# Attention and gated network on one core: part of the weight bit-packing moved to ScalarE, plain products in another order, packs at other places

## The chip, the cores and the metric

The kernel runs on one core of a Trainium2 chip. The metric is the device time of one execution in microseconds (us). The engines are named as in the profile: PE (TensorE matmul), PEld (TensorE weight load), DVE (VectorE), ACT (ScalarE), POOL (GpSimd) and SP (SyncE, which here only issues DMAs). Each engine works through its own instructions in program order.

## The reference

Eight batches, eight heads, 576 positions and head size 64 go through a windowed attention: the first four heads see the last 32 positions, the other four every fourth of the last 128. The result, 4608 rows of 512, goes through a gated network with 1536 inner columns.

```python
scores = scale * np.matmul(q, k.transpose(0, 1, 3, 2))
scores = np.where(masks[None], scores, -1e9)
attn = exp(scores - max) / (sum + 1e-09);  x = (attn @ v)      # rows of 8 heads x 64 = 512
g = x @ w_gate;  silu = g * (1.0 / (1.0 + np.exp(-g)))
val = x @ w_val
out = (silu * val) @ w_out
```

q, k and v are float32; the three weight matrices are float64, and reach the chip as pairs of 32-bit words (a low and a high word).

## The kernel before, in words

**Chunks and steps.** The 4608 rows are twelve chunks of 384 columns (x is held transposed). The first four chunks are "plain": twelve steps each, 48 steps `s` in all, one step for each block of 128 inner columns. A step is 36 matmuls of 128x128 by 128x384: `gv_mm(.., 0)`, the gate, 12 matmuls into the bank `bg` (L401); `gv_mm(.., 1)`, the value, 12 into `bv` (L401); and `out_mm(s - 1)`, the output product of the step before, 12 into four banks `bo` (L439). Every operand is split into a high and a low float32r part, and a product is three matmuls: high by high, high weight by low x, low weight by high x. The last eight chunks run in pairs through a scheme with seven products in place of eight (L713); nothing of the change lies there.

**Between the products of a step.** ACT takes the tanh of the gate (`act_tanh`, L411), DVE multiplies it by the gate (`dve_u`, L416), which frees `bg`, and then by the value (`dve_h`, L421), which frees `bv`; ACT makes the high part of h (`h_hi`, L426) and POOL the low part (`h_lo`, L431), which `out_mm` reads. `bg` and `bv` are single banks, so the gate of step s + 1 waits for `dve_u` of step s, and the value of step s + 1 for `dve_h` of step s.

**Weights.** The weights of a step are two units, 24 units in all, 2s and 2s + 1 for step s. The gate reads unit 2s alone, the value reads both, the output product unit 2s + 1. A unit passes through stages: a load of 768 KB into one of six raw buffers (`w_load`, issued by SP, as soon as the unit that held the buffer has passed stage B); stage E, `w_exp`, on ACT (L205), which rescales the high word in place; stage B, `w_bits`, on DVE, two instructions: the high word shifted left by 3 (L212), then the low word shifted right by 29 and or-ed in (L213); stage H, `w_split_hi`, the float32r high part, on ACT (L221); stage L, `w_split_lo`, the low part, on POOL (L225). All this is done in the first plain chunk; afterwards the weights stay in place.

**What sets the order.** The first four attention packs (chunk 0) and the first units are written out by hand as a string of stages (`first`, for PE, DVE and ACT). After that the steps are written in a loop, in which `w_upto` says up to which unit each stage is written there, and `tc.issue_after` holds the weight work behind `dve_u` or `dve_h`; a scheduler turns what is written into one fixed order for each engine. Attention packs for later chunks are put between the products at numbered slots (`visits`, three slots to a step): a visit "A" computes the results of one pack and the scores of the next, a visit "B" turns them (transposes), and copies x.

## Time and profile before

| | us |
|---|---|
| runs (3): median, lowest, highest | 963.69, 962.80, 965.67 |
| the profiled execution | 964.01 |
| its span, first to last instruction | 962.2 |
| PE busy in the span | 942.5 |
| DVE, ACT, POOL busy | 672.3, 397.7, 375.5 |

The span is 1.8 us shorter than the execution's own time. A busy share is a mean over stages with different limits; the opening (0 to 20 us: attention of chunk 0), the weight stage (20 to 118 us: plain chunk 0 with the 24 units) and all that follows are read apart.

### The profile page before, as it was taken

The numbers are of one execution on the slowest core, as the hardware profiler recorded it, in microseconds if no ns is written. First come the engines' busy times: TensorE is split into PE (matmuls) and PEld (weight loads), VectorE is DVE, ScalarE is ACT, GpSimd is POOL, SyncE is SP. The second block draws the span as 40 slices with busy tenths as digits, with TensorE's granted clock in tenths as the row PEclk, the third lists the DMA queues.
The fourth block names the chain that finished last, engine by engine and source line by source line (L and its number), as shares of the span: only waits on it lengthen the run. The fifth ranks groups of instructions, "written<-read, shape, count | busy, mean of one in ns | idle before, by whom it ended". The sixth has DMA issues, their size and how long they took to land.

```text
span 962.2 us, 23928 instructions
## 1 busy us (share of the span) xinstructions
PE 942.5 (98%) x9960; PEld 915.5 (95%) x9960; DVE 672.3 (70%) x1180; ACT 397.7 (41%) x776; POOL 375.5 (39%) x460
## 2 busy tenths in 40 slices
PE   7899899999999999999999999999999999999998
PEld 6788899999999999999999999999999999999998
DVE  5878655667677655677699487779487789466583
ACT  4664432232333333444546334445334447234352
POOL 1566411111111131334367343455343448354472
PEclk9999999999999999999999999999999999999999
DMA  9774345556766791898979988889988878988873
GB/s 368 304 250 146 129 147 183 195 202 230 242 207 225 240 354 35 262 291 270 294 239 290 344 273 279 259 259 309 333 263 280 275 235 260 307 255 253 258 232 122
DMA packets 86060, 238.12 MB, mean 247 GB/s; under 512 B 8768, under 2 KB 29120, under 8 KB 85952
## 3 DMA queue, kind: packets, MB, share of 16 engines
q0 software_dynamic: 36288, 132.14, 44.1%
q1 hardware_dynamic: 36848, 65.07, 19.1%
q10 hardware_dynamic: 12816, 39.38, 12.3%
q8 instruction: 79, 1.29, 0.6%
q14 instruction: 29, 0.24, 0.1%
HBM read 194.08 MB, written 42.47 MB: 246 GB/s over the span
## 4 chain that ended last, share of the span: by engine, by line
PE 88%; DVE 6%; issue 2%; ACT 2%; DMA 1%; POOL 0%; ACTq 0%; POOLq 0%; SPq 0%; DVEq 0%
PE bo L713 30%; PE bg L713 11%; PE bv L713 11%; PE bv L401 9%; PE bo L439 9%; PE bg L401 9%; PE two L339 3%; PE two L299 2%; DVE at_int L213 1%; PE two L323 1%; PE two L357 1%; DVE at_int L212 1%; DVE at_float32r L672 1%; DMA at_int<-w 1%; ACT at_int L205 1%
## 5 line engine op out<-in xcount | busy, mean ns | idle before, releaser
L713 PE MATMUL bo<-at_float32r,at_float32r 128*128 128x384 f32 x1728 | 318.5, 336 | 0.0
L713 PEld LDWEIGHTS bo<-at_float32r,at_float32r 128*128 128x128 f32 x1728 | 299.8, 188 | 1.0
L645 POOL DMA_DIRECT2D at_float32r<-pieces x252 | 137.8, 547 | 242.4 <-PE bo L713 140.1
L672 DVE TENSOR_TENSOR at_float<-bo,at_float 128x384 f32<-128x384 f32 x224 | 122.0, 552 | 101.5 <-PE bo L713 52.2
L431 POOL TENSOR_TENSOR at_float32r<-at_float,at_float32r 128x384 fp32r<-128x384 f32 x48 | 57.4, 1195 | 214.3 <-PE bo L439 173.6
L713 PE MATMUL bg<-at_float32r,at_float32r 128*128 128x384 f32 x648 | 137.0, 337 | 0.0
L713 PE MATMUL bv<-at_float32r,at_float32r 128*128 128x384 f32 x648 | 136.5, 336 | 0.0
L401 PE MATMUL bv<-at_float32r,at_float32r 128*128 128x384 f32 x576 | 112.5, 342 | 3.0 <-ACT at_float32r L221 1.8
L713 PEld LDWEIGHTS bv<-at_float32r,at_float32r 128*128 128x128 f32 x648 | 114.1, 188 | 0.5
L713 PEld LDWEIGHTS bg<-at_float32r,at_float32r 128*128 128x128 f32 x648 | 113.8, 188 | 0.7
L401 PE MATMUL bg<-at_float32r,at_float32r 128*128 128x384 f32 x576 | 111.5, 340 | 2.7 <-DVE at_float L416 1.2
L439 PE MATMUL bo<-at_float32r,at_float32r 128*128 128x384 f32 x576 | 110.1, 338 | 3.2 <-POOL at_float32r L431 2.9
L672 DVE TENSOR_TENSOR at_float32r<-at_float,at_float32r 128x384 fp32r<-128x384 f32 (+1 forms) x112 | 99.9, 914 | 17.9 <-ACT at_float32r L702 14.0
L702 ACT CAST at_float32r<-at_float 128x384 fp32r<-128x384 f32 x168 | 83.1, 512 | 66.7 <-PE bv L713 22.9
L672 POOL TENSOR_TENSOR at_float32r<-at_float,at_float32r 128x384 fp32r<-128x384 f32 x84 | 91.5, 1090 | 43.9 <-ACT at_float32r L702 42.8
L401 PEld LDWEIGHTS bv<-at_float32r,at_float32r 128*128 128x128 f32 x576 | 100.7, 189 | 5.2 <-ACT at_float32r L221 2.1
L401 PEld LDWEIGHTS bg<-at_float32r,at_float32r 128*128 128x128 f32 x576 | 100.2, 188 | 4.8 <-DVE at_float L416 1.8
L439 PEld LDWEIGHTS bo<-at_float32r,at_float32r 128*128 128x128 f32 x576 | 100.3, 188 | 4.5 <-POOL at_float32r L431 3.5
L739 ACT ACTIVATE at_float<-at_float 128x384 f32<-128x384 f32 x96 | 50.6, 527 | 99.3 <-DVE at_float L672 94.6
L416 DVE SCALAR_TENSOR_TENSOR at_float<-at_float,bg 128x384 f32<-128x384 f32 x48 | 26.5, 552 | 71.5 <-ACT at_float L411 71.5
L718 ACT COPY at_float<-bg 128x384 f32<-128x384 f32 x84 | 40.1, 478 | 81.1 <-PE bg L713 81.0
L672 DVE TENSOR_TENSOR at_float<-at_float,at_float 128x384 f32<-128x384 f32 (+1 forms) x64 | 54.6, 878 | 25.1 <-POOL at_float32r L672 11.3
(78 smaller groups left out, 994.4 us busy)
## 6 DMA issues: line engine op xcount, KB each, us to landing
at_float32r<-pieces POOLq DMA_DIRECT2D x252, 512.0 KB, 4.8
pieces<-at_float32r SPq DMA_DIRECT2D x126, 256.0 KB, 3.5
at_int<-w SPq DMA_DIRECT2D x24, 768.0 KB, 6.2
at_float<-vb ACTq DMA_DIRECT2D x36, 390.0 KB, 5.1
out<-at_float SPq DMA_DIRECT2D x48, 192.0 KB, 4.7
at_float<-qkb ACTq DMA_DIRECT2D x14, 448.0 KB, 6.3
at_float<-qkb ACTq DMA_DIRECT2D x15, 400.0 KB, 5.6
at_float<-qkb ACTq DMA_DIRECT2D x7, 640.0 KB, 6.5
```

What stands on the lines that cost most here:

```text
L299: nc.tensor.matmul(out=two[BQ * j:BQ * j + BQ, h, a + BK * g:a + BK * g + BK], lhsT=t[r, q:q + BQ], rhs=t[r, k:k + BK], start=not masked, ...
L339: nc.tensor.matmul(out=two[BQ * j:BQ * j + BQ, h, (D + 1) * g:(D + 1) * (g + 1)], lhsT=t[r, BQ * i:BQ * i + BQ], rhs=v[r, i, :], start=Tru ...
L401: nc.tensor.matmul(out=bank[:, :CH], lhsT=wcol(f, o, low), rhs=x[k], start=n == 0, stop=n == 3 * NK - 1)
L416: last["h"] = nc.vector.scalar_tensor_tensor(out=t, in0=t, scalar=1.0, in1=bank_g[:, :CH], op0=ALU.add, op1=ALU.mult)
L431: nc.gpsimd.tensor_tensor(out=hl, in0=hst[i][0], in1=hst[i][1], op=ALU.subtract)
L439: nc.tensor.matmul(out=bank_o[j][:, :CH], lhsT=wcol(f, 2 * DM + P * j, low), rhs=x, start=f == 0 and n == 0, stop=f == NF - 1 and n == 2)
L645: nc.gpsimd.dma_start(out=taken[asked], in_=pieces[asked % NPIECE])
L672: engine.tensor_tensor(out=out, in0=a, in1=b, op=op)
L702: nc.scalar.copy(out=o[:, 0], in_=src)
L713: nc.tensor.matmul(out=bank, lhsT=w, rhs=x, start=first and n == 0 and t in FRESH, stop=last and n == len(ops) - 1, skip_group_check=True)
L718: nc.scalar.copy(out=kept[KEPT[t]][r], in_=banks[0][r][:, :CH])
L739: nc.scalar.activation(out=f, in_=g, func=AF.Tanh, scale=0.5)
```

## The change

There are five edits.

1. Stage B is cut in two. A new stage T (`w_shift`) comes ahead of it. For the units 1, 2 and 5, 7, 9 .. 23 (12 of the 24), T is one ACT instruction that multiplies the low word by about 2^-29 and rounds it, in place, and B is a single DVE instruction (high word shifted left by 3, or-ed with the low word). For the other 12 units T and B are the two DVE instructions of before.
2. In `gv_mm` the four matmuls with the low weight part come last, after the eight with the high part.
3. In `out_mm` the eight matmuls with the high part of h come first (two for each bank), the four with the low part of h last.
4. The string of the first stages is written in another order: T and B of unit 0 apart, the results of pack 1 behind the exp of pack 3, unit 2's E earlier, and B of unit 3 and E of units 4 and 5 at the end.
5. The visits of packs 4 to 8 lie at slots 5, 11, 18, 24, 31 (A) and 8, 14, 21, 27, 34 (B) in place of 2, 9, 16, 23, 30 and 6, 13, 20, 27, 33.

```diff
+    STAGES = "ETBHL"
...
-    def w_bits(u):
+    def by_act(u):
+        return u in (1, 2) or u > 3 and u % 2 == 1
+
+    def w_parts(u):
+        return [wst[u][k].rearrange("p (a b) -> p a b", a=3) for k in ("lo", "hi")]
+
+    def w_shift(u):
         n = u - NU + NLAST
         y = at(M_LATE + 4 * WU + YW * (u % 3) if n < 0 else M_SPARE if n == 0 else raw_at[(u + 1) % 4], YW, I32)
...
+        if by_act(u):
+            x = wst[u]["lo"]
+            nc.scalar.activation(out=x, in_=x.bitcast(U32), func=AF.Copy, scale=(1 - 2.0 ** -8) * 2.0 ** -29,
+                                 bias=-0.5 + 7.5 * 2.0 ** -8)
+        else:
+            nc.vector.tensor_scalar(out=wst[u]["y"], in0=w_parts(u)[1], scalar1=3, scalar2=None,
+                                    op0=ALU.logical_shift_left)
+
+    def w_bits(u):
+        y = wst[u]["y"]
+        lo, hi = w_parts(u)
+        if by_act(u):
+            nc.vector.scalar_tensor_tensor(out=y, in0=hi, scalar=3, in1=lo,
+                                           op0=ALU.logical_shift_left, op1=ALU.bitwise_or)
+        else:
+            nc.vector.scalar_tensor_tensor(out=y, in0=lo, scalar=29, in1=y,
+                                           op0=ALU.logical_shift_right, op1=ALU.bitwise_or)
         wst[u] = y
...
     def gv_mm(ci, f, which):
...
-        for j, k in enumerate(ORDER):
+        ops = [(j, 0, x) for j in range(NK) for x in (xh, xl)] + [(j, 1, xh) for j in range(NK)]
...
     def out_mm(i):
...
-        for j in range(4):
-            for n, (low, x) in enumerate(((0, hh), (1, hh), (0, hl))):
+        for j, low, x in [(j, low, hh) for j in range(4) for low in range(2)] + [(j, 0, hl) for j in range(4)]:
...
-        for what in ("Q0 Q1 S0 X0 T0 S1 K0 X1 A0 M0 W0 Q2 N0 T1 K1 S2 X2 Q3 A1 W0 W1 U0 W2 W3 S3 X3 N1 T2 H0 L0 T3 K2 A2 "
-                     "W1 K3 U1 N2 H1 A3 W2 L1 W3 U2 N3 H2 U3 L2 H3 L3 W0 W1 W2 W0 W1").split():
+        for what in ("Q0 Q1 S0 X0 T0 S1 K0 X1 A0 M0 W0 Q2 N0 T1 K1 S2 X2 Q3 W1 W0 S3 X3 A1 U0 N1 W2 T2 K2 H0 L0 W3 W4 "
+                     "T3 A2 K3 W1 U1 N2 A3 H1 L1 W0 W2 U2 N3 W3 H2 U3 L2 W4 H3 L3 W1 W0 W2 W1 W2 W3 W0 W0").split():
...
-        visits(4 + n, 2 + 7 * n, 5 + 7 * n + (n < 4))
+        visits(4 + n, 5 + 13 * n // 2, 8 + 13 * n // 2)
...
-            w_upto(B=W + 5)
+            w_upto(T=W + 5, B=W + 5)
```

What this makes of the order is seen at three places. In the rows, `at_1536_int` are raw weight buffers (in place for E and T), `at_776_int` the packed units, `at_1536_float32r` the split weights and `at_384_float` h. The changed kernel's line numbers are its own: L207 is E, L225 T on ACT, L228 T on DVE, L238 and L235 B (of a unit with T on DVE and on ACT), L246 H, L437 the tanh, L442 `dve_u`, L447 `dve_h`, L452 `h_hi`, L404 the low part of x.

DVE in step 7, from `dve_u` to the next `dve_u`, before:

```order
L416 SCALAR_TENSOR_TENSOR at_384_float_672<-at_384_float_672,bg 128x384
L212 TENSOR_SCALAR at_776_int_362<-at_1536_int_167 128x3x256
L213 SCALAR_TENSOR_TENSOR at_776_int_362<-at_1536_int_167,at_776_int_362 128x3x256
L421 SCALAR_TENSOR_TENSOR at_384_float_672<-at_384_float_672,bv 128x384
L212 TENSOR_SCALAR at_776_int_418<-at_1536_int_173 128x3x256
L213 SCALAR_TENSOR_TENSOR at_776_int_418<-at_1536_int_173,at_776_int_418 128x3x256
```

The same step after the change:

```order
L442 SCALAR_TENSOR_TENSOR at_384_float_630<-at_384_float_630,bg 128x384
L228 TENSOR_SCALAR at_776_int_337<-at_1536_int_167 128x3x256
L238 SCALAR_TENSOR_TENSOR at_776_int_337<-at_1536_int_167,at_776_int_337 128x3x256
L404 TENSOR_TENSOR at_384_float32r<-two,at_384_float32r 128x384
L447 SCALAR_TENSOR_TENSOR at_384_float_630<-at_384_float_630,bv 128x384
L235 SCALAR_TENSOR_TENSOR at_776_int_419<-at_1536_int_173 128x3x256
```

The odd unit's T is gone from DVE; a low part of x stands here now because of the later visit.

ACT around the tanh of step 1 (the second L411), before:

```order
L426 CAST at_384_float32r<-at_384_float_586 128x384
L221 CAST at_1536_float32r<-at_776_int_418 128x768
L205 ACTIVATE at_1536_int_167<-at_1536_int_167 128x768
L411 ACTIVATE at_384_float_672<-bg 128x384
L221 CAST at_1536_float32r<-at_776_int_362 128x768
```

And after:

```order
L452 CAST at_384_float32r<-at_384_float_586 128x384
L225 ACTIVATE at_1536_int_380<-at_1536_int_380 128x768
L246 CAST at_1536_float32r<-at_776_int_419 128x768
L207 ACTIVATE at_1536_int_167<-at_1536_int_167 128x768
L246 CAST at_1536_float32r<-at_776_int_471 128x768
L207 ACTIVATE at_1536_int_173<-at_1536_int_173 128x768
L437 ACTIVATE at_384_float_630<-bg 128x384
```

Ahead of this tanh now stand T of unit 5, H of units 4 and 5 and E of units 6 and 7; before, H of unit 3 and E of unit 6.

ACT around the tanh of step 8, where E of the last two units (22 and 23, raw buffers 167 and 173) stands, before:

```order
L205 ACTIVATE at_1536_int_167<-at_1536_int_167 128x768
L275 DMA at_1280_float_514<-qkb 128x896
L411 ACTIVATE at_384_float_586<-bg 128x384
L319 ACTIVATE at_384_float_850<-at_384_float_850 128x384
L205 ACTIVATE at_1536_int_173<-at_1536_int_173 128x768
```

And after:

```order
L207 ACTIVATE at_1536_int_167<-at_1536_int_167 128x768
L437 ACTIVATE at_384_float_586<-bg 128x384
L308 DMA at_780_float_891<-vb 128x780
L207 ACTIVATE at_1536_int_173<-at_1536_int_173 128x768
L302 DMA at_1280_float_516<-qkb 128x896
L246 CAST at_1536_float32r<-at_776_int_1275 128x768
L346 ACTIVATE at_384_float_887<-at_384_float_887 128x384
```

The exp of pack 7 (L319, L346) stood ahead of E of unit 23 and now stands behind it. The order of SP's DMA issues is the same before and after.

More of the change, by code (lines that the diff above doesn't have):

```diff
@@ L13 @@
 I32 = mybir.dt.int32
+U32 = mybir.dt.uint32
 BF16 = mybir.dt.bfloat16
@@ L205, in w_exp @@
         nc.scalar.activation(out=y, in_=y, func=AF.Prelu, scale=2.0 ** -112, alpha=2.0 ** 32)
-    def w_bits(u):
+    def by_act(u):
[3 more added lines that the diff above has]
+    def w_shift(u):
         n = u - NU + NLAST
         y = at(M_LATE + 4 * WU + YW * (u % 3) if n < 0 else M_SPARE if n == 0 else raw_at[(u + 1) % 4], YW, I32)
-        y = y[:, :3 * (UT + 1)].rearrange("p (a b) -> p a b", a=3)[:, :, :UT]
-        lo, hi = [wst[u][k].rearrange("p (a b) -> p a b", a=3) for k in ("lo", "hi")]
-        nc.vector.tensor_scalar(out=y, in0=hi, scalar1=3, scalar2=None, op0=ALU.logical_shift_left)
-        nc.vector.scalar_tensor_tensor(out=y, in0=lo, scalar=29, in1=y,
-                                       op0=ALU.logical_shift_right, op1=ALU.bitwise_or)
+        wst[u]["y"] = y[:, :3 * (UT + 1)].rearrange("p (a b) -> p a b", a=3)[:, :, :UT]
+        if by_act(u):
[14 more added lines that the diff above has]
+                                           op0=ALU.logical_shift_right, op1=ALU.bitwise_or)
         wst[u] = y
@@ L227, in attention_moe @@
     ready = {"w": False}
-    done = {"E": 0, "B": 0, "H": 0, "L": 0}
+    done = dict.fromkeys(STAGES, 0)
     def w_upto(**to):
@@ L240, in w_one @@
             w_exp(u)
+        elif c == "T":
+            w_shift(u)
         elif c == "B":
@@ L396, in gv_mm @@
         xh, xl = x_hi[ci % 2], x_lo[ci % 2]
-        n = 0
-        for j, k in enumerate(ORDER):
+        ops = [(j, 0, x) for j in range(NK) for x in (xh, xl)] + [(j, 1, xh) for j in range(NK)]
+        for n, (j, low, x) in enumerate(ops):
             o = 4 * P * (j // 2) + 2 * P * which + P * (j % 2)
-            for low, x in ((0, xh), (0, xl), (1, xh)):
-                nc.tensor.matmul(out=bank[:, :CH], lhsT=wcol(f, o, low), rhs=x[k],
-                                 start=n == 0, stop=n == 3 * NK - 1)
-                n += 1
+            nc.tensor.matmul(out=bank[:, :CH], lhsT=wcol(f, o, low), rhs=x[ORDER[j]],
+                             start=n == 0, stop=n == len(ops) - 1)
     hst = {}
@@ L436, in out_mm @@
         _, hh, hl = hst.pop(i)
-        for j in range(4):
-            for n, (low, x) in enumerate(((0, hh), (1, hh), (0, hl))):
-                nc.tensor.matmul(out=bank_o[j][:, :CH], lhsT=wcol(f, 2 * DM + P * j, low), rhs=x,
-                                 start=f == 0 and n == 0, stop=f == NF - 1 and n == 2)
+        for j, low, x in [(j, low, hh) for j in range(4) for low in range(2)] + [(j, 0, hl) for j in range(4)]:
+            nc.tensor.matmul(out=bank_o[j][:, :CH], lhsT=wcol(f, 2 * DM + P * j, low), rhs=x,
+                             start=f == 0 and low == 0 and x is hh, stop=f == NF - 1 and x is hl)
     def out_store(ci):
@@ L494, in attention_moe @@
         "U": lambda m: turn_y(m, x_bank[m]), "H": lambda m: x_copy_hi(m, x_bank[m]),
-        "L": lambda m: x_copy_lo(m, x_bank[m]), "M": lambda m: more_in(), "W": lambda n: w_one("EBHL"[n]),
+        "L": lambda m: x_copy_lo(m, x_bank[m]), "M": lambda m: more_in(), "W": lambda n: w_one(STAGES[n]),
     }
@@ L787, in attention_moe @@
         with tc.issue_after(last["h"].ins):
-            w_upto(B=W + 6)
+            w_upto(T=W + 6, B=W + 6)
         if s > 0:
```

## Prediction

> **What bounds the kernel now.** I read the page's first part, then the busy time by stretches, then who PE waits for, then the groups of the weight stage, then single instructions. The first part (busy us, share of the span, instructions), and the stretches (length; PE, PEld, DVE, ACT, POOL busy; clock, DMA share, GB/s):
>
> ```profile
> PE 942.5 (98%) x9960; PEld 915.5 (95%) x9960; DVE 672.3 (70%) x1180; ACT 397.7 (41%) x776; POOL 375.5 (39%) x460
> ```
>
> ```profile
> 0.00:20.00 20.00, 15.02 (x383) 11.04 (x383) 9.45 (x20) 7.95 (x14) 1.94 (x5) 1.00 0.94 358
> 20.00:118.00 98.00, 86.79 (x1000) 79.33 (x989) 76.92 (x103) 53.49 (x83) 56.41 (x34) 1.00 0.61 221
> 118.00:958.00 840.00, 839.93 (x8589) 824.65 (x8588) 584.86 (x1056) 336.29 (x680) 317.17 (x421) 1.00 0.78 249
> ```
>
> PE is the bound. From 118 us on it never pauses (839.93 of 840), at a granted clock of 1.00, so nothing can be won there but by cheaper matmuls. The change can win the idle 11.2 us (98 - 86.79) of the weight stage and some of the 5.0 us of the opening. Who PE waits for up to 125 us (us in total, times, longest):
>
> ```profile
> PE bo L439 <- POOL at_float32r L431: 2.9, 2, 1.7
> PE bv L401 <- ACT at_float32r L221: 1.8, 1, 1.8
> PE two L323 <- ACT at_float L319: 1.6, 1, 1.6
> PE bg L401 <- DVE at_float L416: 1.2, 2, 1.0
> PE bg L401 <- ACT at_float32r L221: 1.1, 1, 1.1
> PE bv L401 <- POOL at_float32r L225: 0.9, 1, 0.9
> PE two L339 <- ACT at_float L329: 0.8, 1, 0.8
> ```
>
> A dozen waits of one or two us, each behind a different hand-over: no single engine is full, the chains gate, tanh, `dve_u`, B, H, L are late by turns. The groups from 10 to 118 us (count, busy us, mean ns, idle before and releasers) give the prices:
>
> ```profile
> L225 POOL TENSOR_TENSOR at_float32r<-at_int,at_float32r 128x768 fp32r<-128x768 f32 x24 | 42.6, 1778 | 56.9 <-ACT at_float32r L221 56.3
> L213 DVE SCALAR_TENSOR_TENSOR at_int<-at_int,at_int 128x768 int32<-128x768 int32 x24 | 33.7, 1408 | 0.6
> L212 DVE TENSOR_SCALAR at_int<-at_int 128x768 int32<-128x768 int32 x24 | 22.6, 945 | 1.8 <-POOL at_float32r L225 1.4 <-ACT at_int L205 0.2
> L205 ACT ACTIVATE at_int<-at_int 128x768 f32<-128x768 f32 x24 | 21.6, 915 | 10.8 <-DMA at_int<-w 7.1 <-PE fs L299 3.7
> L221 ACT CAST at_float32r<-at_int 128x768 fp32r<-128x768 f32 x24 | 20.1, 835 | 28.4 <-DVE at_int L213 28.3
> L416 DVE SCALAR_TENSOR_TENSOR at_float<-at_float,bg 128x384 f32<-128x384 f32 x11 | 6.1, 551 | 14.1 <-ACT at_float L411 14.1
> ```
>
> The largest chain of waits is POOL on H (L221), H on B (L213): 56.3 and 28.3 us. B varies, and the timeline shows why (start, duration):
>
> ```profile
> 46.32 0.96 DVE L213 SCALAR_TENSOR_TENSOR at_int<-at_int,at_int 128x768 int32<-128x768 int32 x1
> 73.40 1.75 POOL L225 TENSOR_TENSOR at_float32r<-at_int,at_float32r 128x768 fp32r<-128x768 f32 x1 [1.76 <-ACT at_float32r L221]
> 73.81 2.15 DVE L213 SCALAR_TENSOR_TENSOR at_int<-at_int,at_int 128x768 int32<-128x768 int32 x1
> 75.10 1.74 POOL L431 TENSOR_TENSOR at_float32r<-at_float,at_float32r 128x384 fp32r<-128x384 f32 x1
> 116.91 1.01 POOL L431 TENSOR_TENSOR at_float32r<-at_float,at_float32r 128x384 fp32r<-128x384 f32 x1 [2.28 <-ACT at_float32r L426]
> ```
>
> Alone B takes 0.96. Beside L (73.40 to 75.15) it takes 2.15: it ends 0.81 after L. The POOL instruction behind (1.74 in place of 1.01) ends 0.88 after B. So B and POOL exclude each other, each waiting for the whole of the other.
>
> **The change, part by part.** The sum is a walk through the orders of the changed program from 14 us to the first matmul of step 12, each engine in its order, with durations from these rows (E and T on ACT 0.83 net of overlap, H 0.75, T on DVE 0.91, B 0.87, L 1.72, `h_lo` 1.0), B and POOL exclusive, and 12 products 2.08 us. The points compared in the trace of before:
>
> ```profile
> 26.12 1.23 PE L401 MATMUL bv<-at_float32r,at_float32r 128*128 128x384 f32 x6
> ...
> 39.42 2.24 PE L401 MATMUL bg<-at_float32r,at_float32r 128*128 128x384 f32 x12
> ...
> 55.93 2.24 PE L439 MATMUL bo<-at_float32r,at_float32r 128*128 128x384 f32 x12
> ...
> 86.86 2.03 PE L439 MATMUL bo<-at_float32r,at_float32r 128*128 128x384 f32 x10 [1.17 <-POOL at_float32r L431]
> 98.07 2.38 PE L401 MATMUL bg<-at_float32r,at_float32r 128*128 128x384 f32 x12 [1.01 <-DVE at_float L416]
> 105.90 2.00 PE L439 MATMUL bo<-at_float32r,at_float32r 128*128 128x384 f32 x10 [1.74 <-POOL at_float32r L431]
> 122.26 2.28 PE L401 MATMUL bg<-at_float32r,at_float32r 128*128 128x384 f32 x12
> ```
>
> The opening. Before, the exp of pack 3 stood on ACT behind H of unit 0:
>
> ```profile
> 17.76 0.52 ACT L319 ACTIVATE at_float<-at_float 128x384 f32<-128x384 f32 x1
> ```
>
> Now it stands behind E of unit 1 alone, 0.75 earlier, and B of unit 0 has left DVE's way to it. The packs' results follow, and the low part of pack 3's x is ready about 1.0 earlier. Value 0 ends at 26.3 in place of 27.35: 1.05 won.
>
> Steps 0 and 1, to the start of gate 2 (39.4 before). Units 2 and 3 were late (1.1, 1.8, 0.9). Unit 2's H now ends at 26.85. But the first waits have successors: gate 1 waits 0.85 for `dve_u`, which DVE has behind T of unit 3; value 1 waits 0.7 for `dve_h`, which stands behind a B that waits for L of unit 2; low parts cost 0.45. The largest one is new: the tanh of step 1 now stands behind H of unit 5, whose B waits twice for POOL (34.0 to 34.85), and behind E of unit 7. It runs at 36.5, `dve_u` ends at 37.45, and gate 2 waits 2.7 for its bank. Gate 2 starts at 37.5, another 0.85 won.
>
> Steps 2 and 3, to the end of output 2, pack 4's results and pack 5's scores (58.1 before). The exp of pack 4 (1.6) still comes late, by 1.1; the copy behind it (0.8) has 25 matmuls more before it is needed. DVE has one T less in each step. The walk reaches the point at 54.2: 2.0 won.
>
> Steps 4 to 6 and 7: 0.6 won with no wait of note. Output 6 (1.17 lost to `h_lo`): the low part of h is needed six matmuls later, 1.04 us, and comes earlier too: 1.2 won.
>
> Steps 8 to 11. Here two raw buffers decide. E of units 22 and 23 stands on ACT ahead of tanhs and waits for its load, which starts when B of units 18 and 19 ends. The page's median of such a load (us to landing) and, in the chain of waits, that of unit 23, with two products of plain chunks 1 and 2 for later:
>
> ```profile
> at_int<-w SPq DMA_DIRECT2D x24, 768.0 KB, 6.2
> ```
>
> ```profile
> 94.17 7.24 DMA at_int<-w
> ...
> 138.53 2.12 PE bv L401 x12
> ...
> 216.74 2.08 PE bv L401 x12
> ```
>
> B of unit 18 ends at 83.6, so unit 22 is there at 89.8, and of the 1.01 before gate 9 at most 0.4 is left. Unit 23 (B of 19 ends at 87.05) lands at 94.3, and the exp of pack 7 stands behind its E: the transposes behind that run at 96.4, whatever gate 9 did, after a wait of about 2. Output 8's `h_lo` (1.74 and 0.24) no longer holds PE. Value 9 starts at 96.75, and gate 10, to which before lost 2.0 more, at 101.2. Net 0.8 won.
>
> 1.05 + 0.85 + 2.0 + 0.6 + 1.2 + 0.8 = 6.5 us; gate 12 starts at 115.8 in place of 122.3, and nothing after is longer. The profiled execution took 964.0, which gives 957.5; the median of the runs is 0.3 lower (963.7), so I say 957.3, between the two.
>
> What costs nothing there, and its cover. Twelve ACT instructions more (10 us): ACT is busy 53.5 of 98, and waits 28.3 for B. If each came on the path, the ten after unit 2 would cost 8.3. T leaves DVE twelve times: 11.3 us, but DVE waited 14.1 for tanh already, so only the part in the chains counts. The visits' moves: pack 7's x must be there at gate 12; its transpose now stands behind value 11 in place of ahead of it, which leaves 18 matmuls (3.1 us) to its use, and ACT and DVE need 1.7 of them. SP's order is unchanged.
>
> Unknown prices. The new ACT instruction converts integers both ways, and no row shows one. Nearest is E: same tile, in place, same stride, 0.915. Below it the CAST (0.835); above I take twice E, 1.83, since a conversion could need a second pass. I take 0.915. The new order of plain products: twelve take 2.12 in chunk 1 and 2.08 in chunk 2; if the order inside the twelve decides that, the 48 gates and values of two chunks are 1.9 us to either side. I take 0, since the same order had both values.
>
> The rows say that B waits for a whole POOL instruction. The Trainium skill, page "SBUF — State Buffer", section "Who interferes with whom", says the same of DVE instructions with two SBUF inputs against GpSimd's reads, and that one-input instructions stay clear; by that rule the instruction removed (L212, one input) never held POOL, the 24 that remain all can, and the sum stays 957.3. The trace agrees: 0.945 for L212 throughout, 1.408 for L213. If it were a mere slowing, each B at its mean, the walk would lose its 2.7 before gate 2, and the sum would be 954.6.
>
> **Rivals.** *The port eats it* (same). Exclusive use in a step is two L, two B and one `h_lo`: 3.44 + 1.74 + 1.0 = 6.2, as much as PE's 6.24 without attention. If every B waits as at 73.81, 2.15, DVE's 24 cost 17.8 more than now (24 x 0.74) against 11.3 removed; the waits of step 1 repeat in each step, and only the opening and the two `h_lo` waits are won: 1.05 + 2.2, less about 1: 962. For it: 56.41 of POOL's time lies in the stage. Against it: POOL waits 56.3 for H, so there are gaps. Chance 0.12.
>
> *ACT becomes the bound* (slower). At 1.83 each, T puts 0.92 more in front of the tanh of each step from 1 to 10: 9.2 us, minus 6.5, is 2.7 slower, 966.4. It decides from 1.57 us for one instruction (0.92 and a tenth of 6.5). For it: the orders put T of odd units ahead of tanhs 1, 5, 6 and 7. Against: the ACT rows of 768 elements take 0.84 to 0.92. Chance 0.04.
>
> *All waits go* (faster still): the tanh of step 1 and unit 23 are not late on the chip. 2.7 and 2.2 fewer: 952.4. For it: each rests on an order of events closer than 1 us. Chance 0.15.
>
> *The split does nothing*: the waits go only because packs moved. This would give the same time and shows only in where DVE waits.
>
> **How the numbers follow.** My forecast has 0.69; its own range is 955 to 960. The range runs from the third rival to the first, 953.3 to 961.8. 0.3% is 2.9 us, about what a measurement of this kernel tells from no change: faster means below 960.8. That is the forecast (0.67 of its 0.69) and the third rival, 0.82; same is the first rival and the rest, 0.14; slower 0.04.
>
> **What the profile after would show.** PE from 118 us on as now; idle before it about 5 us less in the weight stage. L212's successor 12 times at 0.94, the new ACT instruction 12 times at 0.92. Gate 2 released by DVE after a late tanh; a wait of pack 7's transposes on the exp behind unit 23's load. No PE wait on L431. Output products of 2.08 us. I am wrong if the ACT row is above 1.2, if POOL's wait on H falls without PE's idle time falling, or if twelve products leave 2.08 to 2.12.

## The result, and the profile after

The changed kernel took 953.81 us (median of 5 runs, 953.26 to 954.83) where the kernel before took 964.78 beside it (5 runs, 962.8 to 966.94): a ratio of 0.9886, 95% interval 0.9868 to 0.9905, 11.0 us faster. The profiled execution took 953.3 with a span of 951.4, 10.7 less than before's 964.0. The forecast was 957.3 in a range of 953.3 to 961.8: the sign and the range held, the range by 0.5 us at its low end, and the sum of 6.5 us was 4.2 too small.

Line numbers of the changed file that are needed below, beside those given with the change: L is L250, gates and values L428, `h_lo` L457, outputs L465; of the packs, scores L326, exp L346, transposes of e L350, copy behind them L356, results L366 and transposes of y L384.

The first part of the page after, and the stretches (length; PE, PEld, DVE, ACT, POOL busy; clock, DMA share, GB/s), cut at 108 us, since the weight stage ends earlier now:

```profile
PE 939.0 (99%) x9960; PEld 914.2 (96%) x9960; DVE 653.7 (69%) x1168; ACT 406.6 (43%) x788; POOL 376.8 (40%) x460
```

```profile
0.00:20.00 20.00, 14.57 (x387) 10.74 (x388) 8.81 (x21) 8.16 (x15) 0.81 (x5) 1.00 0.93 359
20.00:108.00 88.00, 84.49 (x991) 79.54 (x991) 60.45 (x91) 62.59 (x95) 57.96 (x35) 1.00 0.69 246
108.00:947.00 839.00, 838.93 (x8582) 823.26 (x8581) 583.32 (x1055) 335.89 (x679) 318.08 (x421) 1.00 0.78 249
```

PE is still the bound, and behind the stage nothing changed: 838.93 busy of 839.00. The whole gain lies in the first 125 us. "Gate s" is the gate product of step s. Gates 1 (in two pieces), 2 and 12, to be set against before's 28.73, 39.42 and 122.26:

```profile
27.61 1.63 PE L428 MATMUL bg<-at_float32r,at_float32r 128*128 128x384 f32 x8 [0.63 <-DVE at_float L442]
30.00 0.97 PE L428 MATMUL bg<-at_float32r,at_float32r 128*128 128x384 f32 x4 [0.76 <-POOL at_float32r L250]
35.87 1.31 PE L428 MATMUL bg<-at_float32r,at_float32r 128*128 128x384 f32 x6 [0.74 <-DVE at_float L442]
...
111.06 2.28 PE L428 MATMUL bg<-at_float32r,at_float32r 128*128 128x384 f32 x12
```

Gate 12 starts 11.2 us earlier. From it to the end of the span before took 839.9 and after 840.3: 0.4 given back. Who PE still waits for (us in total, times, longest):

```profile
PE bg L428 <- DVE at_float L442: 1.4, 2, 0.7
...
PE two L350 <- ACT at_float L346: 0.8, 1, 0.8
PE bg L428 <- POOL at_float32r L250: 0.8, 1, 0.8
```

Of before's seven rows from 0.8 to 2.9 us five are gone; the wait for `dve_u` (1.2) and the one for pack 4's exp (1.6) are left at 1.4 and 0.8, and the one for POOL (L of unit 2) has grown from 0.3 to 0.8. All three lie ahead of 47 us; nearly all of PE's other idle time is in the opening. Added over the timeline, PE idles 8.9 us up to gate 12 where it idled 16.2. That is 7.3 of the 11.2. The other 3.9 sit inside groups that the trace calls busy: the same 144 matmuls of `bv` up to gate 12 count 28.1 us in place of 29.7, and the 132 of `bo` 25.2 in place of 25.9. A table of idle time alone would have missed a third of the gain.

1.4 of these 3.9 lie in the opening: up to the end of value 0, PE was busy for 22.4 us before and for 21.0 after with the same 466 matmuls. The stretches print a clock of 1.00 there, but the trace has no clock record ahead of 21.9 us in before and ahead of 16.3 us in after, and the durations show a slower PE. The same three transposes, in before ahead of and behind 21.9 us, and in after:

```profile
20.08 0.90 PE L357 MATMUL fx<-at_float,at_float 128*128 128x128 f32 x3
22.74 0.55 PE L357 MATMUL fs<-at_float,at_float 128*128 128x128 f32 x3
...
19.54 0.55 PE L384 MATMUL fx<-at_float,at_float 128*128 128x128 f32 x3
```

In the traces that do have a record there (e_act_early, from 14.3 to 21.1 us) it says 0.50, and three transposes take 0.90 as well. So PE came to its full clock 5.6 us earlier in after than in before. In the four traces with the old first string the last rise to 1.00 ahead of 23 us lies at 21.9 to 22.5, in the ten with the new one at 15.9 to 21.2.

The groups from 10 to 110 us (count, busy us, mean ns, idle before, releasers):

```profile
L250 POOL TENSOR_TENSOR at_float32r<-at_int,at_float32r 128x768 fp32r<-128x768 f32 x24 | 45.8, 1915 | 40.0 <-ACT at_float32r L246 39.8
L246 ACT CAST at_float32r<-at_int 128x768 fp32r<-128x768 f32 x24 | 20.0, 833 | 9.6 <-DVE at_int L238 6.4 <-DVE at_int L235 3.0
L235 DVE SCALAR_TENSOR_TENSOR at_int<-at_int 128x768 int32<-128x768 int32 x12 | 15.1, 1262 | 0.6 <-ACT at_int L225 0.6
L238 DVE SCALAR_TENSOR_TENSOR at_int<-at_int,at_int 128x768 int32<-128x768 int32 x12 | 11.9, 989 | 0.2
L228 DVE TENSOR_SCALAR at_int<-at_int 128x768 int32<-128x768 int32 x12 | 11.4, 948 | 0.1
L225 ACT ACTIVATE at_int<-at_int 128x768 int32<-128x768 uint32 x12 | 11.0, 920 | 0.0
L442 DVE SCALAR_TENSOR_TENSOR at_float<-at_float,bg 128x384 f32<-128x384 f32 x12 | 6.7, 554 | 22.5 <-ACT at_float L437 22.5
```

The lateness moved as the change meant it to: H waits 9.4 for B (28.3 before), L waits 39.8 for H (56.3), and DVE, which was the late one, now waits 22.5 for the tanh (14.1). B fell from 1408 ns to 989 in the DVE units and 1262 in the ACT units.

### The profile page after: what moved, and what is told of

Its sections match the earlier page's. It is cut to its first block, busy times and chain, and to the rows that moved or that the text cites. A ratio compares the mean times of both kernels' runs of the same rounds, so it can differ in the third digit from the quotient of the medians.

```text
span 951.4 us, 23933 instructions
## 1 busy us (share of the span) xinstructions
PE 939.0 (99%) x9960; PEld 914.2 (96%) x9960; DVE 653.7 (69%) x1168; ACT 406.6 (43%) x788; POOL 376.8 (40%) x460
## 4 chain that ended last, share of the span: by engine, by line
PE 93%; DVE 4%; ACT 2%; issue 1%; DMA 0%; ACTq 0%; DVEq 0%
PE bo L739 31%; PE bg L739 11%; PE bv L739 11%; PE bo L465 10%; PE bv L428 10%; PE bg L428 10%; PE two L366 3%; PE two L326 3%; PE two L350 2%; PE two L384 2%; DVE at_float32r L698 1%; DVE at_float L698 0%; DMA at_bfloat<-masks 0%; ACT at_float32r L246 0%; ACT at_int L207 0%
## 5 line engine op out<-in xcount | busy, mean ns | idle before, releaser
L457 POOL TENSOR_TENSOR at_float32r<-at_float,at_float32r 128x384 fp32r<-128x384 f32 x48 | 55.6, 1158 | 216.5 <-PE bo L465 169.5
L739 PEld LDWEIGHTS bv<-at_float32r,at_float32r 128*128 128x128 f32 x648 | 114.0, 188 | 0.5
L428 PE MATMUL bg<-at_float32r,at_float32r 128*128 128x384 f32 x576 | 111.5, 340 | 2.1 <-DVE at_float L442 1.4
L428 PE MATMUL bv<-at_float32r,at_float32r 128*128 128x384 f32 x576 | 110.8, 339 | 0.0
L465 PE MATMUL bo<-at_float32r,at_float32r 128*128 128x384 f32 x576 | 109.4, 337 | 0.0
L428 PEld LDWEIGHTS bg<-at_float32r,at_float32r 128*128 128x128 f32 x576 | 100.3, 188 | 3.9 <-POOL at_float32r L250 1.1
L428 PEld LDWEIGHTS bv<-at_float32r,at_float32r 128*128 128x128 f32 x576 | 100.4, 188 | 0.9
L465 PEld LDWEIGHTS bo<-at_float32r,at_float32r 128*128 128x128 f32 x576 | 100.4, 188 | 0.5
L442 DVE SCALAR_TENSOR_TENSOR at_float<-at_float,bg 128x384 f32<-128x384 f32 x48 | 26.6, 554 | 77.6 <-ACT at_float L437 77.6
```

The source lines that it names most:

```text
L428: nc.tensor.matmul(out=bank[:, :CH], lhsT=wcol(f, o, low), rhs=x[ORDER[j]], start=n == 0, stop=n == len(ops) - 1)
L442: last["h"] = nc.vector.scalar_tensor_tensor(out=t, in0=t, scalar=1.0, in1=bank_g[:, :CH], op0=ALU.add, op1=ALU.mult)
L457: nc.gpsimd.tensor_tensor(out=hl, in0=hst[i][0], in1=hst[i][1], op=ALU.subtract)
L465: nc.tensor.matmul(out=bank_o[j][:, :CH], lhsT=wcol(f, 2 * DM + P * j, low), rhs=x, start=f == 0 and low == 0 and x is hh, stop=f == NF - ...
L739: nc.tensor.matmul(out=bank, lhsT=w, rhs=x, start=first and n == 0 and t in FRESH, stop=last and n == len(ops) - 1, skip_group_check=True)
```

## The experiments

The change has three parts: T of twelve units on ACT (A), the low parts last in the plain products (P), and the places of units and packs (S, the first string and the visits). With before and after, six kernels make all eight combinations. The others go into one part.

One thing holds for nearly all of them: the scheduler writes the fixed order anew for each kernel, so that an edit also moves instructions that it does not name. ACT's order around the first tanh, from the traces:

| kernel | ACT in order |
|---|---|
| before | E E tanh E H E `h_hi` |
| A alone | E T E E H E tanh E T H E `h_hi` |
| after | T E tanh H E E H `h_hi` |
| e_act_more | T E T H E E H tanh T E `h_hi` |

What a run gives is thus the worth of an edit together with the order that came of it. P alone (ACT and DVE in the order of before) and e_act_early (the order of after but for its T's and the place of one E) are the cleanest.

### All but one part

Kernel e_no_act (P and S):

```diff
     def by_act(u):
-        return u in (1, 2) or u > 3 and u % 2 == 1
+        return False
```

> The kernel after with every unit's lower word brought down on DVE again (no ACT part); the order of products and the places stay new. Theory (the units' chains through T, B, H and L end last, and the places alone can't take DVE's load away): most waits of the weight stage come back, gate 12 starts 3 to 5 us later than the 111.06 of after, time 957 to 959. Rival 'the split does nothing': gate 12 at 111, time 953.8 as after. Rival 'the parts add up': about 3 to 4 us of the 11 are lost, 957 to 958, and the same part alone in the kernel before would win as much.

Kernel e_old_products (A and S):

```diff
-        ops = [(j, 0, x) for j in range(NK) for x in (xh, xl)] + [(j, 1, xh) for j in range(NK)]
+        ops = [(j, low, x) for j in range(NK) for low, x in ((0, xh), (0, xl), (1, xh))]
...
-        for j, low, x in [(j, low, hh) for j in range(4) for low in range(2)] + [(j, 0, hl) for j in range(4)]:
+        for j, low, x in [(j, low, x) for j in range(4) for low, x in ((0, hh), (1, hh), (0, hl))]:
```

> The kernel after with the plain products in their old order (low part of x or h between the others). Theory: the low parts are ready late in several gates, values and outputs (each six matmuls, 1.04 us, later in the new order), and PE waits on POOL or DVE for them again: 2 to 4 us lost, 956 to 958, products of 12 as now 2.08 to 2.12. Rival 'product order does all': the waits all come back, 961 or more. Rival 'the parts add up': as the theory. If the order inside twelve products has a price of its own, the stretch from gate 12 on (840.3 in after) changes by up to 1.9 us.

Kernel e_old_places (A and P): the first string of before, and

```diff
-        visits(4 + n, 5 + 13 * n // 2, 8 + 13 * n // 2)
+        visits(4 + n, 2 + 7 * n, 5 + 7 * n + (n < 4))
```

> The kernel after with the old first string and the old visits of the packs. Theory: the exp of pack 3 stands behind H of unit 0 again, which loses the 1.05 us of the opening, and the later packs cost 1 to 2 us more, 956 to 957.5. Rival 'the split does nothing' (all is won by places): 960 or more. Rival 'the parts add up': 955 to 957.

### One part alone

Kernels e_only_act, e_only_products and e_only_places are the changed file with the two other parts undone by the same edits.

> The kernel before with the ACT part alone: old order of products, old places, T just ahead of its B. The four kernels so far gave: without the ACT part 961.2, with old places 961.5, with old products 956.6, with all parts 953.8, against 963.4. The losses 7.4, 7.7 and 2.8 sum to 17.9 where all parts together won 9.6, so the parts don't add up. Theory (T on ACT and the places need each other: ACT's time for T must be free ahead of the tanhs and exps, and the places make it so): the ACT part alone wins nothing to 2 us, 961.5 to 963.5, with PE waits behind tanh and dve_u as large as those it removes. Rival (each alone does most of the work): 957 to 959.

> The kernel before with the order of products alone. Theory: what this part wins does not hang on the others, since it only moves the need of a low part back by six matmuls: 1.9 to 2.8 us won as between the kernels so far, 960.6 to 961.5, and no PE wait on the POOL instruction of output 6 and 8. Rival (the chains move on into the next wait): nothing, 963.

> The kernel before with the new first string and visits alone. Theory: without T on ACT, DVE stays late and the places win nothing to 1 us, 962.4 to 963.4. Rival 'the split does nothing': 956 or less.

What the eight gave. The ratio is to the kernel before on the same chip, with its 95% interval; gate 12, the largest single wait of PE from 20 to 125 us and the time at a granted clock of 0.50 from 23 to 125 us are from each profile, that is from one execution (of A alone the slowest of eleven, 964.1; of P and S together the fastest of ten, 960.0):

| parts | median us | ratio | gate 12 | largest wait | at 0.50 |
|---|---|---|---|---|---|
| none (before) | 963.4, 964.5 | 1 | 122.3 | 1.80 | 0 |
| A | 962.6 | 0.9970 [0.9955, 0.9984] | 121.4 | 3.69 | 6.8 |
| P | 963.9 | 0.9992 [0.9982, 1.0002] | 120.8 | 2.49 | 3.4 |
| S | 964.4 | 0.9994 [0.9982, 1.0005] | 121.9 | 5.55 | 10.2 |
| A, P | 961.5 | 0.9967 [0.9953, 0.9981] | 120.0 | 3.57 | 3.4 |
| P, S | 961.2 | 0.9970 [0.9956, 0.9983] | 117.5 | 3.57 | 3.4 |
| A, S | 956.6 | 0.9930 [0.9915, 0.9944] | 114.4 | 1.85 | 0 |
| A, P, S (after) | 953.8 | 0.9886 [0.9868, 0.9905] | 111.1 | 0.80 | 0 |

Alone A wins 0.3%, and P and S cannot be told from no change; together the three win 1.1%. A and S together win twice what they win apart (0.70% against 0.30 + 0.06), and P, worth 0.08% alone, is worth 0.44% on top of both. "The split does nothing" has fallen: without A the time is 961.2. So has "product order does all", and the parts do not add up. From gate 12 to the end all eight take 839.9 to 840.9, so everything is decided ahead of it.

Why one part alone wins so little is seen in its trace. With A alone, on ACT and PE (start, duration):

```profile
26.70 1.69 ACT L207 ACTIVATE at_int<-at_int 128x768 f32<-128x768 f32 x2
28.27 0.83 ACT L246 CAST at_float32r<-at_int 128x768 fp32r<-128x768 f32 x1
28.99 0.90 ACT L207 ACTIVATE at_int<-at_int 128x768 f32<-128x768 f32 x1
29.77 0.49 ACT L437 ACTIVATE at_float<-bg 128x384 f32<-128x384 f32 x1
...
31.45 3.20 PE L428 MATMUL bg<-at_float32r,at_float32r 128*128 128x384 f32 x12 [3.69 <-DVE at_float L442]
```

The first tanh, which ran at 26.50 before and runs at 26.20 in after, stands here behind three E and an H, at 29.77, and gate 1 waits 3.69. The T ahead of it took 0.9 of this; the rest is the place that the scheduler gave the tanh. With A and P it is the same, 3.57. With S alone, on DVE and PE:

```profile
48.86 2.13 DVE L238 SCALAR_TENSOR_TENSOR at_int<-at_int,at_int 128x768 int32<-128x768 int32 x1
50.91 0.68 DVE L340 TENSOR_REDUCE at_float<-two 128x8 f32<-128x512 f32 x1
...
53.02 1.11 PE L350 MATMUL two<-at_float,at_float 128*128 128x128 f32 x4 [5.55 <-ACT at_float L346]
```

Pack 4's first DVE instruction waits behind two pairs of T and B, the second B at 2.13 beside L, and PE waits 5.55 for the exp behind it. In after the same reduction runs at 43.08, right behind `dve_h`. So each part by itself moves the lateness into one long wait (P too, 2.49). S goes with DVE relieved by A, and A with a string in which the tanh comes ahead of the E's; whether A with the old string and the tanh put ahead by hand would do as well was not run.

A long wait can cost twice. The stretches of e_no_act around its wait of 3.57 (the figure behind POOL's is the clock):

```profile
48.00:50.00 2.00, 0.00 (x0) 0.00 (x0) 1.58 (x3) 1.18 (x2) 2.00 (x2) 1.00 0.84 335
50.00:52.00 2.00, 1.67 (x7) 1.67 (x8) 0.00 (x0) 2.00 (x4) 2.00 (x2) 0.50 1.00 331
52.00:54.00 2.00, 2.00 (x10) 2.00 (x9) 1.23 (x2) 1.54 (x3) 0.54 (x1) 0.65 0.77 299
54.00:56.00 2.00, 2.00 (x13) 2.00 (x13) 1.82 (x4) 0.69 (x2) 0.00 (x0) 1.00 0.06 23
```

Behind the wait the granted clock is 0.50, then 1.00 again; it is at half for 3.41 us, which takes 1.7 us of PE's work. From 22 us on the profile of before never left 1.00, and neither did the one of after. e_no_act and e_old_places came out 2 and 4 us above what was expected of them; one wait of 3.57 and 1.7 for the clock behind it, which each of them has, were not in the estimate.

For the products, without P the two waits that grow are those behind the tanh and at pack 4's transposes (A and S):

```profile
38.15 2.35 PE L428 MATMUL bg<-at_float32r,at_float32r 128*128 128x384 f32 x12 [1.43 <-DVE at_float L442]
...
48.91 0.66 PE L350 MATMUL two<-at_float,at_float 128*128 128x128 f32 x4 [1.85 <-ACT at_float L346]
```

and hardly any wait on a low part itself (0.3 at output 0; the 0.7 at gate 1 for L of unit 2 is in after too). What P wins with A and S in place is won in steps 0 to 3 (gate 4 starts at 56.09 without it and at 52.76 in after, gate 12 at 114.40 and 111.06), so the expectation had the size (2.8 in 2 to 4) but not the place. P alone was expected at 960.6 to 961.5 and gave 963.9, a miss: value 1 waits 2.49 for H, and the clock is at half from 35.9 to 39.3.

### The places divided

Kernel e_old_visits: after with the line `visits(4 + n, ...)` of before, and the new first string.

> The kernel after with the old visits of the packs from step 2 on, and the new first string. It divides the 7.7 us of the places. With all old places the trace had 3.6 of wait before gate 1, and 0.6, 0.7, 1.3 and 0.7 in outputs 6 and 8, at both packs that the visits put there. Theory: the waits in outputs 6 and 8 are the visits' and the wait at gate 1 is the string's, so about 3.2 us are lost here, 956.5 to 957.5. Rival: the string alone decides, since it sets how far PE is ahead in the stage: 954.

957.58 us (ratio 0.9924, 0.9911 to 0.9937): 3.8 more than after, where 3.2 was worked out. Gates 1 and 2 run as in after (27.57 and 35.85). The largest new waits are in output 8:

```profile
97.07 1.69 PE L465 MATMUL bo<-at_float32r,at_float32r 128*128 128x384 f32 x8 [1.40 <-ACT at_float32r L452]
99.43 0.96 PE L465 MATMUL bo<-at_float32r,at_float32r 128*128 128x384 f32 x4 [0.67 <-POOL at_float32r L457]
```

These two are 2.1 of the 3.7 us by which gate 12 is late against after; 0.5 more is a wait of gate 9 for `dve_u`, and the rest is spread. Output 6, expected to wait too, does not. The other half of the places, 961.5 to 957.6, is the first string's, with the wait of 3.57 before gate 1. The string alone does not decide.

### ACT's part doubled

Kernel e_act_twice: the one instruction as two, with the same result.

```diff
-            nc.scalar.activation(out=x, in_=x.bitcast(U32), func=AF.Copy, scale=(1 - 2.0 ** -8) * 2.0 ** -29,
+            nc.scalar.activation(out=x, in_=x.bitcast(U32), func=AF.Copy, scale=(1 - 2.0 ** -8) * 2.0 ** -1)
+            nc.scalar.activation(out=x, in_=x.bitcast(U32), func=AF.Copy, scale=2.0 ** -28,
                                  bias=-0.5 + 7.5 * 2.0 ** -8)
```

> The kernel after with each of the twelve new ACT instructions done as two, in place, with the same result (0.92 us more of ACT per unit, 11 us in all). Theory: ACT has idle time in the stage (62.6 busy of 88 from 20 us on) and the chains have slack at most units, so 1 to 3 us are lost, where T stands ahead of a tanh: 955 to 957. Rival 'ACT becomes the bound' as it was priced ahead of the result: 0.92 for each of ten steps, 9.2 us, 963. A price of nothing would say that every T on ACT lies in idle time.

965.6 us (ratio 1.0014, 1.0002 to 1.0026): the whole gain is gone, and my expectation of 1 to 3 us with it. 10.9 us of ACT time were added, and 11.8 came back. The rival of the prediction, "ACT becomes the bound", had priced 0.92 more per step at 9.2 for ten steps, which is near. Its mechanism is not what the trace shows: ACT is no fuller from 20 to 50 us, 23.8 busy of 30 where after has 25.3, and PE's waits are spread over `dve_u`, the exps, `dve_h` and `h_hi`. The groups of DVE show that the loss is not ACT's time alone:

```profile
L236 DVE SCALAR_TENSOR_TENSOR at_int<-at_int 128x768 int32<-128x768 int32 x12 | 16.0, 1337 | 12.0 <-POOL at_float32r L458 10.8 <-ACT at_int L226 1.2
L239 DVE SCALAR_TENSOR_TENSOR at_int<-at_int,at_int 128x768 int32<-128x768 int32 x12 | 15.7, 1309 | 0.1
```

B of the DVE units is back at 1309 ns (989 in after): B falls beside L again. PE idles 17.1 us up to gate 12, against 8.9, and 1.7 more went to a stretch at half clock at 104 us. ACT's order differs from after's too, so the price of one more instruction by itself is not shown; what is shown is that the idle time of ACT covered none of it.

Its eleven executions fall into groups by their mean granted clock: the four at 0.999 or 1.000 have spans of 962.3 to 962.6, the five at 0.998 spans of 963.5 to 964.3 (the other two, at 0.992 and 0.993, 963.7 and 963.8). If the 0.998 is one half-clock stretch in the weight stage, as in the execution that was profiled, it is worth about 1.5 us by these, beside the 1.7 from the trace.

### Which units, and E

Three kernels change only the rule of `by_act`; the fourth changes E's place in the steps:

```diff
-        return u in (1, 2) or u > 3 and u % 2 == 1
+        return u in (1, 2, 5, 7, 9)          # e_act_early
+        return u > 9 and u % 2 == 1          # e_act_late
+        return u == 2 or u % 2 == 1          # e_act_more
...
-        w_upto(L=W + 3, H=W + 4, E=W + 6)
+        w_upto(L=W + 3, H=W + 4, E=W + 5)    # e_exp_late
-        w_upto(L=W + 4, H=W + 5, E=W + 7)
+        w_upto(L=W + 4, H=W + 5, E=W + 6)    # e_exp_late
```

> The kernel after with only the units 1, 2, 5, 7 and 9 brought down on ACT; units 11 to 23 as before on DVE. In after PE has no wait from 50 us on (30.00 busy of 30, 28.00 of 28), and units 11 to 23 are brought down from about 50 us on. Theory (ACT's relief of DVE is needed where PE waits, in steps 0 to 3, and the rest lies in idle time): 954 to 955.5, no more than 1.5 us behind after. Rival (it is needed in every step, since DVE's B beside POOL takes up to 2.1): 957 to 960.

> The kernel after with units 1, 2, 5, 7 and 9 on DVE as before and only units 11 to 23 on ACT. Theory: pack 4's transposes wait 3.6 for the exp behind two pairs of T and B on DVE, with a stretch of half clock behind that, as in the kernel without the ACT part: 959.5 to 961.5. Rival (needed in every step): 956 to 958.

> The kernel after with unit 3 on ACT too and unit 1 still there (13 units). Two ACT instructions per unit cost 11.8 us in all, nearly their whole duration, so ACT has little to give between 20 and 50 us (25.3 busy of 30). Theory: the 0.9 more on ACT stands ahead of gate 1's tanh or H of unit 2 and comes back as 0.5 to 1.5 us lost, 954.3 to 955.5. Rival (DVE is still the late one there): up to 1 us won, 952.8 to 953.8.

> The kernel after with E of each unit from step 0 on one unit later in the written order, so that in most steps an E no longer stands ahead of the tanh. The doubled ACT part showed that ACT's time ahead of tanh is what costs. Theory: the waits before gate 2 (0.74) and at pack 4's transposes (0.80) go or shrink, 952.5 to 953.8. Rival (E is then late itself for its T and B, and the raw buffers come free later): 954 to 957.

The kernel before took 964.8 beside these.

| kernel | median us | ratio | gate 12 | largest wait |
|---|---|---|---|---|
| e_act_early | 956.0 | 0.9911 [0.9894, 0.9929] | 113.2 | 1.08 |
| e_act_late | 959.7 | 0.9947 [0.9931, 0.9962] | 117.8 | 3.58 |
| e_act_more | 957.1 | 0.9920 [0.9904, 0.9937] | 114.3 | 3.79 |
| e_exp_late | 956.6 | 0.9909 [0.9892, 0.9927] | 114.0 | 2.74 |

The five early units carry most of it: with them alone 956.0, without them 959.7. That is between the theory (at most 955.5) and the rival (957 at least), nearer the theory; the later units are worth about 2 us at most, 1.08 of it in a wait at 92.5 us that after does not have. 0.34 of the 2.1 us by which gate 12 is late here stand already at value 0 and gate 2 (36.22 against 35.87), where the two programs are the same: they come from the opening's clock, not from the units. e_act_late repeats the long wait of e_no_act at pack 4's transposes, with 6.8 us at half clock behind it.

e_act_more and e_exp_late were tries at a better version; both lost. In e_act_more, on ACT:

```profile
25.94 0.91 ACT L225 ACTIVATE at_int<-at_int 128x768 int32<-128x768 uint32 x1
26.72 0.85 ACT L246 CAST at_float32r<-at_int 128x768 fp32r<-128x768 f32 x1
27.45 1.71 ACT L207 ACTIVATE at_int<-at_int 128x768 f32<-128x768 f32 x2
29.02 0.85 ACT L246 CAST at_float32r<-at_int 128x768 fp32r<-128x768 f32 x1
29.75 0.52 ACT L437 ACTIVATE at_float<-bg 128x384 f32<-128x384 f32 x1
```

One T more, and the scheduler put the first tanh behind two H and two E that in after stand behind it: it runs at 29.75, not 0.92 later than 26.20 but 3.55. Later E's did remove the wait before gate 2, as expected, but pack 4's transposes then wait 2.74, behind a B of 2.44 on DVE.

No version that beats the changed kernel was found.

## Why the prediction held, and which terms were mis-sized

**The number: too small, and saved by the range.** 953.8 lies outside the forecast's own range of 955 to 960, and 0.5 us inside the whole one, whose low end was said to be the third rival's, though that rival's own figure is 952.4. So the way and the place of the gain were forecast; that the range held owes something to luck, and two terms of the sum had a wrong size.

**What bounds, and where it can win: right.** PE, from 22 us on at a clock of 1.00, and only ahead of gate 12. But I named the idle 11.2 us of the stage and some of the opening's 5.0 as all that could be won, and 3.9 of the gain came out of time booked as busy, 1.4 of them in the opening; the walk by starts of gates, which made the sum, counts that too.

**The walk.** Its points against after, each with what it had won:

| point | before | forecast | after |
|---|---|---|---|
| end of value 0 | 27.35 | 26.3 | 26.97 |
| gate 2 | 39.42 | 37.5 | 35.87 |
| gate 4, behind output 2 and pack 5's scores | 58.0 | 54.2 | 52.76 |
| gate 10 | 107.75 | 101.2 | 96.55 |
| gate 12 | 122.26 | 115.8 | 111.06 |

*The opening, 1.05 forecast, 0.4 measured.* The exp came 0.7 earlier as worked out, and new waits behind it gave it back:

```profile
17.66 0.55 PE L350 MATMUL fs<-at_float,at_float 128*128 128x128 f32 x3 [0.66 <-ACT at_float L346]
...
19.10 0.51 PE L366 MATMUL fr<-at_float,at_float 64*32 64x65 f32 x34 [0.62 <-issue]
```

Even the 0.4 can't be put down to the exp. In e_act_early, the same program up to there, the clock came up at 21.1 us in place of 16.3, and value 0 ended at 27.33, where before has 27.35. The forecast had no term for the clock of the opening.

*Steps 0 and 1, 0.85 forecast, 3.2 measured* (39.42 - 35.87, less 0.4). This is the first of two mis-sized terms: the wait before gate 2, forecast 2.7, measured 0.74. The walk let B of unit 3 wait for L of unit 2. On the chip B came first:

```profile
26.91 0.55 DVE L442 SCALAR_TENSOR_TENSOR at_float<-at_float,bg 128x384 f32<-128x384 f32 x1
27.37 0.95 DVE L238 SCALAR_TENSOR_TENSOR at_int<-at_int,at_int 128x768 int32<-128x768 int32 x1
27.49 4.89 POOL L250 TENSOR_TENSOR at_float32r<-at_int,at_float32r 128x768 fp32r<-128x768 f32 x2 [2.50 <-ACT at_float32r L246]
28.24 0.55 DVE L447 SCALAR_TENSOR_TENSOR at_float<-at_float,bv 128x384 f32<-128x384 f32 x1
...
34.76 0.47 ACT L437 ACTIVATE at_float<-bg 128x384 f32<-128x384 f32 x1
```

B started 0.12 ahead of L and took 0.95; the two L's took 4.89 in place of 3.44. So `dve_h` was in time (no wait of 0.7 at value 1), and the low part of gate 1 paid 0.76. B of unit 5 waited for POOL once (31.08 to 33.19) where the walk had a second time, 34.0 to 34.85; H of unit 5 ran at 33.22, and the second tanh at 34.76, not 36.5.

*Steps 2 and 3, 2.0 forecast, 1.7 measured* (58.0 - 52.76, less 3.55): right, its wait for the exp of pack 4 0.80 where 1.1 was worked out.

*From there to gate 12, 0.6 + 1.2 + 0.8 = 2.6 forecast, 6.0 measured* (11.2 - 5.25). The waits on `h_lo` are gone as forecast. The second mis-sized term is the lateness of the two raw buffers: about 2 at pack 7's transposes and up to 0.4 before gate 9 were charged, and neither wait exists:

```profile
79.95 0.96 DVE L238 SCALAR_TENSOR_TENSOR at_int<-at_int,at_int 128x768 int32<-128x768 int32 x1
81.75 0.95 DVE L235 SCALAR_TENSOR_TENSOR at_int<-at_int 128x768 int32<-128x768 int32 x1
85.14 0.91 ACT L207 ACTIVATE at_int<-at_int 128x768 f32<-128x768 f32 x1 [1.57 <-DMA at_int<-w]
88.95 0.91 ACT L207 ACTIVATE at_int<-at_int 128x768 f32<-128x768 f32 x1 [2.52 <-DMA at_int<-w]
91.00 0.53 ACT L346 ACTIVATE at_float<-at_float 128x384 f32<-128x384 f32 x1 [0.44 <-DVE at_float L341]
...
92.05 0.49 PE L350 MATMUL two<-at_float,at_float 128*128 128x128 f32 x3
```

B of units 18 and 19 ended at 80.9 and 82.7, not 83.6 and 87.05. E of unit 23 did wait for its load and started 6.2 behind that B, which is the median that was used (unit 22's came 4.2 behind its B); but at 88.95, not 94.3, and ACT had the exp of pack 7 done at 91.53, before PE asked for it. The price of the load was right and the hour of B was wrong: 1.4 of the 4.4 us of B's lateness were already in the walk at gate 4; the rest I put down to turns of B and POOL that the walk had and the chip had not, which no run took apart.

With these three terms put right (2.7 to 0.74, 2.4 to 0, the opening 0.65 less) the walk gives 6.5 + 2.0 + 2.4 - 0.65 = 10.2 of the 11.2; 1.0 stays unassigned, and 0.4 is given back behind gate 12.

**The unknown prices: right.** The integer instruction on ACT took 0.920 (0.915 taken, 0.835 to 1.83 as bounds). Products of twelve kept 2.08 to 2.12; from gate 12 on the kernels with the old order have 839.9 to 840.5 and those with the new order 840.3 to 840.9; either order has two values, 0.6 apart, so up to 0.4 is the order's, where 0 was taken and 1.9 allowed. DVE's T took 0.948 in the mean of twelve. None of the three signs of being wrong showed.

**The rivals.** *All waits go* (952.4, given 0.15) is what came nearest: both waits that it named, of the second tanh and of unit 23, went or shrank to 0.74, and the profiled execution took 953.3. The forecast and this rival have the same mechanism and differ in two orders of events, and in both the forecast took the wrong one: B of unit 3 came before L of unit 2, by 0.12 us, and the exp of pack 7 before PE's need, by 0.5. *The port eats it* fell: B still falls beside L in after (2.11 us from 31.08, ending 0.81 behind L, the same 0.81 as in the pair that was read before), so the exclusion stands, but B's mean fell in all units. *ACT becomes the bound* fell: the instruction takes 0.92. Doubled, it costs what the rival worked out, though not by a full ACT. *The split does nothing* fell to e_no_act and e_only_places, as far as these can be told from the orders that the scheduler made of them.

**What was missing altogether.** I priced each part as if it kept its worth by itself, and had no term for PE's clock. From 22 us on neither hurt the sum, because after has no wait above 0.80 there; in the opening the clock's share is as large as what was won; both would have spoiled a forecast of any one part.

## What to carry to other kernels

Where many waits of one or two us stand behind different hand-overs, a change of one engine's load or order alone may only join them into one long wait: forecast the parts together, by a walk through the starts of the bound engine's work, and test them by undoing one at a time from the full change as well as by adding one at a time to the old kernel. Where a scheduler sets the order, compare the orders first: an edit of one instruction can move a dozen others. Count what one more instruction does ahead of a tanh or an exp: ACT had 25.3 busy of 30 us, and still 10.9 us more of it, in the order that came of it, cost 11.8. In a walk with two engines that exclude each other, give both orders of any meeting closer than about 0.2 us a price, and carry both to the end.

## What the hardware showed that was not expected

**A wait of PE can be followed by 3.41 us at half the clock.** From 23 us on it was seen behind single waits of 2.49, 2.74 and 3.57 to 3.79, behind 1.54 and 0.69 close together (S alone), behind one of 1.74 (A alone, below) and one of 1.75 (e_act_twice), and for twice as long behind 5.55 and, in e_act_late, 3.58; not in the profiles of before and after. One kernel, A alone, shows both outcomes for the same work behind waits of almost the same length:

```profile
85.58 2.03 PE L465 MATMUL bo<-at_float32r,at_float32r 128*128 128x384 f32 x10 [1.73 <-POOL at_float32r L457]
...
103.52 2.85 PE L465 MATMUL bo<-at_float32r,at_float32r 128*128 128x384 f32 x10 [1.74 <-POOL at_float32r L457]
```

Behind the first the clock stays at 1.00; behind the second it is 0.50 from 104.4 to 107.8, and the ten matmuls take 2.85 in place of 2.03. The Trainium skill, page "TensorE: Matmul & The Clock Gate", section "Part 1: The HAM clock gate (the "warmup" mystery)", speaks of a free-running window of about 3.4 us and of half rate after an idle window; the traces agree with the window's length and the half rate, and show that a window need not be idle throughout.

The traces say more. In each of them the clock changes only at times that lie a whole number of 3.413 us apart, so each has a fixed grid of windows, at another place in every execution. PE's busy time in some windows at a clock of 1.00, and the clock in the next:

| kernel | window, us | PE busy in it, us | clock in the next |
|---|---|---|---|
| S alone | 48.10 to 51.51 | 0.00 | 0.50 |
| P alone | 32.47 to 35.88 | 1.22 | 0.50 |
| S alone | 27.62 to 31.03 | 1.40 | 0.50 |
| A alone | 100.99 to 104.40 | 1.50 | 0.50 |
| before | 103.81 to 107.22 | 1.67 | 1.00 |
| A alone | 83.92 to 87.33 | 1.75 | 1.00 |
| e_old_visits | 96.11 to 99.52 | 1.78 | 1.00 |
| before | 32.13 to 35.54 | 1.82 | 1.00 |

Over all fourteen traces there are 411 such windows between 22 and 125 us: the eleven with PE busy for at most 1.51 us are followed by half the clock, and the 400 with 1.67 or more are not. So what decides here is how much of a wait falls into one window, not its length. The two waits of the pair differ by that: 1.66 us of the first lie in one window, and of the second all 1.74 with 0.17 of a smaller wait. Before's 1.80 and 0.86 lie in two windows, 1.82 and 2.35 busy. At half clock, two windows with 1.91 and 1.97 us busy were followed by another at half, behind 5.55 and in e_act_late; those with 3.08 or more by 1.00. The border was read from the traces afterwards, on one kind of load; in the opening, with its small matmuls, one window of 1.77 busy was followed by half clock too. No run was made that moves a wait against the grid.

**An integer conversion on ACT costs what a float pass costs.** 128x768 from uint32 to int32 in place took 920 ns, against 915 for E on the same shape.
